# Two MLPs behind an attention: the last product in seven products too, and a weight matrix turned by VectorE

## The chip, the cores and the metric

One core of one Trainium2 chip. The metric is the time of one execution in device microseconds (us), as the median of several runs. A profile is one execution, recorded instruction by instruction; its span runs from the first to the last instruction. The engines have short names in it: PE is TensorE, DVE is VectorE, ACT is ScalarE, POOL is GpSimd, SP is SyncE, which issues nearly all DMAs.

## What is computed

```python
def reference(q, k, v, w_in, w_out, w1, w2, w3, w_out2):
    x = windowed_attention(q, k, v)         # 4 x 8 heads x 576 x 64 -> 2304 tokens x 512
    h = x @ w_in                            # 512 -> 2048
    x = np.maximum(0.01 * h, h) @ w_out     # 2048 -> 512
    a = x @ w1                              # 512 -> 1024
    b = x @ w2
    h = a * b @ w3                          # 1024 -> 1024
    return h @ w_out2                       # 1024 -> 512
```

The inputs q, k and v come in single precision, the weights in double. A product in single precision is made of three matmuls, of high and low parts: with a = a_hi + a_lo, the terms are lo x hi, hi x lo and hi x hi (`mm3`, line 124, matmuls on lines 126 to 128). The high part is a rounding copy and the low part a subtraction, the two steps of `split_steps` (line 115).

## The kernel before

The program goes through stages, each with TensorE work in it. Attention and first MLP share the time up to about 350 us, the first MLP running on to about 550 us. Beside the first MLP's last parts lie two more stages.

**The fold of w3** (about 346 to 432 us). Since (a*b) w3 w_out2 = (a*b)(w3 w_out2), the kernel computes wp = w3 w_out2 once, 1024x512. w3 comes in 16 blocks of 128x512 double-precision words. `conv3` turns each into single precision (POOL, ScalarE and VectorE, tile `wf` with its second half-word in `rf`), and `keep_w3` (line 654) turns it by four TensorE transposes of 128x128 into a PSUM bank (`ps_w3T`, line 661). It is then split into high and low (`w3T`), VectorE making the low part. `split_wo2` (line 640) splits the rows of w_out2 (`wo`), `fold_steps` (line 674) multiplies into four banks `ps_wp`, `store_steps` (line 683) copies these out and stores them in DRAM. The order of all this is written by hand: each letter of the string `START` (line 928) is one step of one stage, emitted on whatever engines it uses, and the string `LOADS` orders SP's loads. The engines run their own queues in that order and meet at semaphores.

**The weight sums** (to about 550 us), `weight_sums`, make for the gates the sums of blocks of w1 and w2 that a 2x2 product in seven products wants, and store them in DRAM (`ws_dram`). `split_wp` (line 777, letters `,` and `;`) splits wp here, 8 times.

**The second MLP** (551.8 us to the end, loop at line 1086) is what the change is about. It runs three passes; a pass has 768 tokens, two chunks of 384. A pass has eight gates. `Gate` (line 784) computes for 128 of the 1024 features both a and b, for both chunks: a 2x2 block product of weights and tokens in seven products rather than eight, numbered 1, 5, 2, 6, 7, 3, 4 in their order. Each has six matmuls 128x384. They read `ys`, seven tiles of token sums and parts for this pass (`sum_y_steps`, line 754; `ysum` a sum, then a split of 128x768), and `ws`, the weight sums. Intermediate sums stay in the banks a, b, c, e; ScalarE copies between them, VectorE does the additions and the product a*b, ScalarE and POOL split the result (`keep`, line 800) into `p`, the stationary operand of the final product. The next gates' first products are emitted between the last products of the gate before.

`final_part` (line 840) is the final product: for each of the 18 token tiles of 128 tokens 8 x 3 matmuls 128x512 (`ps_y`) of p with wp, a copy by ScalarE (line 852) and one DMA of 128 rows of 2 KB (line 854); the last tile goes in two halves of 256 columns. At the end of a pass the sums `ys` of the next pass are emitted two by two between those token tiles.

Of the kernel before, what the change touches and what calls it, by code (L numbers as in the profile page):

```python
# [28 lines left out]
def tile_window_attention_two_mlps(  # L29
# [14 lines left out]
    nc = tc.nc  # L44
# [100 lines left out]

    def shift(w):
        nc.vector.tensor_scalar(w, w, 3, None, op0=ALU.logical_shift_left)
        yield

    def to_float32(raw, w, r, e_t, shifted=False):  # L150
# [4 lines left out]
        yield  # L155
        halves = r.bitcast(I16).rearrange("p (n two) -> p n two", two=2)
# [35 lines left out]
    class Convert:  # L192
# [3 lines left out]
        def __init__(self, jobs, raw_tile, w_tile, r_tile, pats):  # L196
            self.jobs, self.raw_tile, self.w_tile, self.r_tile = jobs, raw_tile, w_tile, r_tile
            self.raws, self.fetched, self.made, self.done, self.pats = {}, 0, 0, None, pats
            self.ws = {}
# [21 lines left out]

        def block(self):
            i = self.made
            self.made = i + 1
            w, r = self.w_tile(i), self.r_tile(i)
            self.ws[i] = w
            e = [engine_of[x] for x in self.pats[i % len(self.pats)]]
            yield from to_float32(self.raws.pop(i), w, r, e[0], shifted=True)
# [362 lines left out]
    def evacuate_steps(c, f, f0, f1):  # L591
        n = CH[c][1]
        x2 = x2_parts(c)
        if f == f1 - 1:
            for i in range(2):
# [11 lines left out]
                else:  # L607
                    for j in range(2):
                        if c == NCH - 1:
                            if j == 0:  # L610
                                st6 = fin.tile([P, 2, MT], F32, tag="p", name=f"st{c}_{i}", bufs=2 * NI)
# [15 lines left out]
    def load_w3(raw, src, i):  # L627

        r0, c0 = i // (NI // NG) * NG * P, i % (NI // NG) * 2 * P
        nc.sync.dma_start(  # L630
            raw.rearrange("p (c f) -> p c f", c=NG),
            src[r0 : r0 + NG * P, c0 : c0 + 2 * P].rearrange("(c p) f -> p c f", p=P),
        )
# [20 lines left out]
    def keep_w3(i):  # L654


        def finish(w, e_hi, e_lo):
            ps = bank(f"ps_w3T{i}")
            for j in range(2):
                for c in range(NG):  # L660
                    nc.tensor.transpose(
                        ps[:, (j * NG + c) * P : (j * NG + c + 1) * P],
                        w[:, (c * 2 + j) * P : (c * 2 + j + 1) * P], ident,
                    )
# [3 lines left out]
            yield from split_steps(  # L668
                t[:, 0], t[:, 1], ps.rearrange("p (j r) -> p j r", j=2), e_hi, e_lo
            )  # L670
# [12 lines left out]
    def store_steps(g):  # L683
        for x in range(NG):
            st = st_t[:, x * 2 * HS[0] :][:, :DM]
            copy_on(nc.scalar if x % 2 else nc.vector)(st, wp_ps[g][x])
# [5 lines left out]
    yf, ys, pr = {}, {}, {}  # L692
# [61 lines left out]
    def sum_y_steps(p, k):  # L754
        b11, b21, b12, b22 = (yf[2 * p + c][:, 2 * a : 2 * a + 2] for c in range(2) for a in range(2))
        s = {0: b11, 2: b21, 4: b22}.get(k)
        if s is None:
            if k == 1:
                ysum[0] = pre.tile([P, 2, MT], F32, tag="ysum", name=f"ysum{p}", bufs=1)
            if k == 5:  # L760
                ysum[1] = fin.tile([P, 2, MT], F32, tag="ysum", name=f"ysum{p}_5", bufs=1)
            s = ysum[k == 5]
# [5 lines left out]
        yield from split_steps(t[:, 0], t[:, 1], s, nc.scalar, nc.vector)  # L768
# [4 lines left out]
    def load_wp(ib):  # L773
        wp[ib] = wo_slot(f"wps{ib}")
        nc.sync.dma_start(wp[ib][:, 1].bitcast(F32), wp_dram[ib * P : (ib + 1) * P, :])

    def split_wp(ib):
        t = wp[ib]
        yield from split_steps(t[:, 0], t[:, 1], t[:, 1].bitcast(F32), nc.scalar, nc.vector)

    def one(tag, name):
        return banks.tile([P, 512], F32, tag=tag, name=name, bufs=2)

    class Gate:
# [3 lines left out]
        def __init__(self, p, i):  # L788
            self.p, self.i = p, i

        def product(self, k, ps, seeded=False):
            x, j, of = PRODUCT[k]
            w = ws[self.p, self.i, x][:, j]
# [3 lines left out]
        def temp(self, name):  # L797
            return fin.tile([P, MT], F32, tag=name, name=f"{name}{self.p}_{self.i}", bufs=2)

        def keep(self, c, g):  # L800
            t = fin.tile([P, 2, MT], F32R, tag="p", name=f"p{2 * self.p + c}_{self.i}", bufs=2 * NI)
            split(t[:, 0], t[:, 1], g, nc.scalar, nc.gpsimd)
            pr[2 * self.p + c, self.i] = t

        def first(self):
            name = f"{self.p}_{self.i}"
            self.a = one("a", f"ps_a{name}")[:, :MT]
            self.product(1, self.a)
            self.b = one("b", f"ps_b{name}")[:, :MT]
            nc.scalar.copy(self.b, self.a)  # L810

        def second(self):
            self.e = one("e", f"ps_e{self.p}_{self.i}")[:, :MT]
# [7 lines left out]
            self.c = one("c", f"ps_c{self.p}_{self.i}")[:, :MT]  # L821
            nc.scalar.copy(self.c, self.b)

        def third(self):
# [9 lines left out]
            self.product(4, self.b, seeded=True)  # L834
            tt(self.c11, self.c11, self.b, op=ALU.mult)
            self.keep(0, self.c11)

    ps_y = {}

    def final_part(c, tb, i0, i1, cols=None):  # L840
        x, n = cols or (0, DM)
        if i0 == 0:
            ps_y[c, tb, x] = one("a", f"ps_y{c}_{tb}_{x}")[:, :n]
        ps = ps_y[c, tb, x]
        for i in range(i0, i1):
            mm3(
# [310 lines left out]
```

## Time and profile before

| | us |
|---|---|
| median of 3 runs (lowest, highest) | 830.77 (830.13, 831.62) |
| the profiled execution | 830.42 |
| its span | 828.6 |
| TensorE busy | 816.0 (98%) |
| VectorE busy | 426.8 (52%) |
| ScalarE busy | 413.2 (50%) |
| POOL busy | 206.4 (25%) |
| share of TensorE in the chain of work that ended last | 93% |

Busy time of TensorE counts matmuls that overlap in the array; what a matmul costs the queue is the distance between two starts. The views by window show the stages, the timeline the starts, and the groups by line and shape the durations on the other engines.

### The profile page before, as it was taken

What the parts mean: (1) busy time and instruction counts of PE and PEld (TensorE: products, weight loads), DVE (VectorE), ACT (ScalarE), POOL (GpSimd) and SP (SyncE); (2) the same over time, 40 slices, a digit from 0 to 9 for tenths busy, and PEclk for the clock granted to TensorE, in tenths of its full rate; (3) what the DMA queues carried; (4) which work ended last, traced back from release to release, by engine and by line L of the source; (5) the groups of instructions that cost most, each with busy time, mean ns of one, the idle gap of its engine ahead of it and who ended that gap; (6) DMA issues with size and microseconds to landing.
All of it is one profiled execution on the core that took longest, in us unless ns stands there. A gap on an engine that the chain in (4) does not pass through costs nothing.

```text
span 828.6 us, 15344 instructions
## 1 busy us (share of the span) xinstructions
PE 816.0 (98%) x5816; PEld 776.9 (94%) x5816; DVE 426.8 (52%) x852; ACT 413.2 (50%) x929; POOL 206.4 (25%) x236
## 2 busy tenths in 40 slices
PE   7999999999999999999999999999999999999998
PEld 6799899999999999989989999999998999899987
DVE  4999997553645364564653768752324233233310
ACT  3899882452134343565654778654423443334411
POOL 4514521333433143422212200002210121002210
PEclk9999999999999999999999999999999999999999
DMA  6995837346444441465746889749731885158001
GB/s 141 274 321 185 264 102 200 99 141 185 109 137 100 100 107 30 156 215 178 228 141 222 271 286 346 246 150 325 255 97 51 326 293 181 44 202 253 22 26 51
DMA packets 104569, 146.37 MB, mean 177 GB/s; under 512 B 44720, under 2 KB 70064, under 8 KB 104496
## 3 DMA queue, kind: packets, MB, share of 16 engines
q1 hardware_dynamic: 104496, 145.39, 55.9%
q8 instruction: 46, 0.75, 0.4%
q14 instruction: 27, 0.22, 0.1%
HBM read 115.87 MB, written 29.49 MB: 175 GB/s over the span
## 4 chain that ended last, share of the span: by engine, by line
PE 93%; SPq 2%; DVE 2%; ACT 1%; issue 1%; DMA 1%; POOL 0%; DVEq 0%; ACTq 0%; POOLq 0%
PE ps_h L126 8%; PE ps_x L126 8%; PE ps_x L127 8%; PE ps_x L128 8%; PE ps_h L128 8%; PE ps_h L127 8%; PE ps_y L128 4%; PE ps_y L127 4%; PE ps_y L126 4%; PE ps_b L128 3%; PE ps_b L126 3%; PE ps_b L127 3%; PE ps_s L402 2%; PE ps_o L488 2%; PE ps_a L126 2%; PE ps_a L128 2%
## 5 line engine op out<-in xcount | busy, mean ns | idle before, releaser
L126 PE MATMUL ps_h<-x,win 128*128 128x384 f32 (+2 forms) x448 | 143.1, 319 | 1.0 <-ACT g L539 1.0
L128 PE MATMUL ps_h<-x,win 128*128 128x384 f32 (+2 forms) x448 | 140.0, 313 | 0.0
L127 PE MATMUL ps_h<-x,win 128*128 128x384 f32 (+2 forms) x448 | 140.0, 312 | 0.0
L126 PE MATMUL ps_x<-gs,wout 128*128 128x384 f32 (+2 forms) x356 | 114.7, 322 | 0.0
L128 PE MATMUL ps_x<-gs,wout 128*128 128x384 f32 (+2 forms) x356 | 112.4, 316 | 0.0
L127 PE MATMUL ps_x<-gs,wout 128*128 128x384 f32 (+2 forms) x356 | 112.4, 316 | 0.0
L118 POOL TENSOR_TENSOR gs<-g,gs 128x384 fp32r<-128x384 f32 (+2 forms) x69 | 65.3, 947 | 147.7 <-DVE gs L116 141.9
L539 ACT ACTIVATE g<-ps_h 128x384 f32<-128x384 f32 (+2 forms) x112 | 49.3, 440 | 104.4 <-PE ps_h L128 67.7
L118 POOL TENSOR_TENSOR p<-u,p 128x384 fp32r<-128x384 f32 x24 | 24.4, 1015 | 270.6 <-ACT p L116 238.8
L126 PEld LDWEIGHTS ps_h<-x,win 128*128 128x128 f32 x448 | 84.6, 189 | 3.3 <-ACT g L539 1.5
L127 PEld LDWEIGHTS ps_h<-x,win 128*128 128x128 f32 x448 | 84.6, 189 | 0.3
L128 PEld LDWEIGHTS ps_h<-x,win 128*128 128x128 f32 x448 | 84.5, 189 | 0.0
L829 DVE TENSOR_TENSOR u<-u,ps_e 128x384 f32<-128x384 f32 x24 | 13.3, 554 | 136.3 <-ACT u L828 136.3
L126 PEld LDWEIGHTS ps_x<-gs,wout 128*128 128x128 f32 x356 | 67.1, 189 | 1.0
L127 PEld LDWEIGHTS ps_x<-gs,wout 128*128 128x128 f32 x356 | 67.2, 189 | 0.2
L128 PEld LDWEIGHTS ps_x<-gs,wout 128*128 128x128 f32 x356 | 67.1, 189 | 0.0
L128 PE MATMUL ps_y<-wps,p 128*128 128x512 f32 (+1 forms) x152 | 57.5, 379 | 0.0
L127 PE MATMUL ps_y<-wps,p 128*128 128x512 f32 (+1 forms) x152 | 57.5, 379 | 0.0
L126 PE MATMUL ps_y<-wps,p 128*128 128x512 f32 (+1 forms) x152 | 57.4, 378 | 0.0
L116 DVE CAST gs<-g 128x384 fp32r<-128x384 f32 (+2 forms) x70 | 24.7, 352 | 62.5 <-PE ps_x L128 52.5
L128 PE MATMUL ps_b<-ys,ws 128*128 128x384 f32 x144 | 48.1, 334 | 0.0
L126 PE MATMUL ps_b<-ys,ws 128*128 128x384 f32 x144 | 48.1, 334 | 0.0
(157 smaller groups left out, 1902.8 us busy)
## 6 DMA issues: line engine op xcount, KB each, us to landing
ws<-ws_dram SPq DMA_DIRECT2D x63, 512.0 KB
raw<-in_moe_w_out_dram SPq DMA_DIRECT2D x24, 512.0 KB
ws_dram<-ws SPq DMA_DIRECT2D x24, 512.0 KB
raw<-in_moe_w_in_dram SPq DMA_DIRECT2D x16, 512.0 KB
rawf<-in_moe_w_dram SPq DMA_DIRECT2D x16, 512.0 KB
wo2f<-wo_dram SPq DMA_DIRECT2D x32, 256.0 KB
rawl<-in_moe_w_dram SPq DMA_DIRECT2D x16, 512.0 KB
q<-in_q_dram SPq DMA_DIRECT2D x48, 140.0 KB
```

The source lines that it names most:

```text
L116: copy_on(e_hi)(hi, src)
L118: e_lo.tensor_tensor(lo, src, hi.bitcast(F32), op=ALU.subtract)
L126: nc.tensor.matmul(ps, a[1], b[0], start=first, stop=False, skip_group_check=seeded)
L127: nc.tensor.matmul(ps, a[0], b[1], start=False, stop=False, skip_group_check=seeded)
L128: nc.tensor.matmul(ps, a[0], b[0], start=False, stop=last, skip_group_check=seeded)
L402: nc.tensor.matmul(ps[j * QB : (j + 1) * QB, i - bl.start], qt[d, i * QB : (i + 1) * QB], kt[d, first_key(i, plain) : first_key(i, plain) ...
L488: nc.tensor.matmul(ps[j * D : (j + 1) * D, i * QB : (i + 1) * QB], vt[i][:, h + j, :], t[:, i, j * QB : (j + 1) * QB], start=True, stop=True,)
L539: nc.scalar.activation(g, ps, AF.Prelu, alpha=SLOPE)
L829: tt(u3, u3, self.e, op=PLUS)
```

## The change

**The final product in seven products.** Each pass is cut into two halves of four gates, and each half's final product is made for two column halves d, as a 2x2 block product (class `Final`): the blocks are the feature halves of a pair of gates (even and odd) by the two chunks on the one side, blocks of wp on the other. Its result stands transposed, output features on partitions and 384 tokens along the row. So the gates keep no longer a*b of two chunks but seven sums of pairs of gates (`Gate.keep` with keys 1 to 7; the differences by VectorE, the low parts of 1, 5, 7, 4, 3 by POOL, of 6 and 2 by VectorE). The first half's results are kept in `yacc` (four tiles) and added in the second half, four additions a half by POOL, the others by VectorE. The output tile is turned back by VectorE's 32x32 transpose and written in pieces of 256 bytes, 384 pieces to a DMA, four DMAs to a tile.

**The parts of wp** for it (`fold_sums`) are sums and splits of four blocks of 256 rows and lie in the first half of the first pass; `split_wp` is gone. Lists `urgent` and `spare` (`behind`, `need`) hold the steps that stand beside the products, one list item being begun behind each product.

**The gates** change a little: bank c is b + m5 by VectorE rather than a copy by ScalarE, u is b + m5 by VectorE. The weights for later gates come in a ring of 16 slots of 256 KB, 16 products ahead.

**w3** is loaded in bands of 32 rows and turned by VectorE's transpose, 16 instructions of 128x512, into `rf`; w_out2 is stored from bands that suit it, and the copies in `store_steps` are cut in two with the columns reordered. `START` and `LOADS` are changed in some letters.

The core of the diff:

```diff
+        for b in range(P // E):
+            nc.sync.dma_start(
+                raw[b * E : (b + 1) * E].rearrange("x (r f) -> x r f", f=2 * E),
+                rows(
+                    src, r0 * F2 + c0 + b * 2 * E,
+                    [[F2, E], [E * F2, NG * P // E], [1, 2 * E]],
+                ),
+            )
...
         def finish(w, e_hi, e_lo):
-            ps = bank(f"ps_w3T{i}")
-            for j in range(2):
-                for c in range(NG):
-                    nc.tensor.transpose(
-                        ps[:, (j * NG + c) * P : (j * NG + c + 1) * P],
-                        w[:, (c * 2 + j) * P : (c * 2 + j + 1) * P], ident,
-                    )
+            turned = conv3.rs[i].bitcast(F32).rearrange("p (j r x) -> p r j x", j=2, x=E)
+            nc.vector.transpose(turned, w.rearrange("p (r j y) -> p r j y", j=2, y=E))
             yield
...
     def sum_y_steps(p, k):
...
+        e_lo = nc.gpsimd if p and k in LO_ON_POOL else nc.vector
...
-        yield from split_steps(t[:, 0], t[:, 1], s, nc.scalar, nc.vector)
+        yield from split_steps(t[:, 0], t[:, 1], s, nc.scalar, e_lo)
+
+    LO_ON_POOL = (0, 2, 4, 5)
...
         def third(self):
             tt = nc.vector.tensor_tensor
             self.product(7, self.b, seeded=True)
             u3 = self.temp("u3")
-            nc.scalar.copy(u3, self.b)
-            tt(u3, u3, self.e, op=PLUS)
+            tt(u3, self.b, self.m5, op=PLUS)
+            behind()
             self.product(3, self.c, seeded=True)
-            tt(self.m5, self.m5, self.c, op=PLUS)
-            tt(u3, u3, self.m5, op=ALU.mult)
-            self.keep(1, u3)
+            behind()
+            tt(u3, u3, self.c, op=ALU.mult)
+            odd = self.i % 2
+            if odd:
+
+                t1, u3e = raw["t1"], raw["u3"]
+                self.keep(6, t1, nc.vector, (t1, u3, t1))
             self.product(4, self.b, seeded=True)
+            behind()
             tt(self.c11, self.c11, self.b, op=ALU.mult)
-            self.keep(0, self.c11)
...
+            if odd:
+                self.keep(2, self.c11, nc.vector)
+                self.keep(7, u3e, nc.gpsimd, (u3e, u3, u3e))
+                self.keep(4, t1, nc.gpsimd, (t1, self.c11, t1))
+                self.keep(3, u3, nc.gpsimd)
+            else:
+                raw["u3"] = u3
+                raw["t1"] = t1 = self.temp("t1", 1)
+                self.keep(1, self.c11, nc.gpsimd)
+                self.keep(5, t1, nc.gpsimd, (t1, u3, self.c11))
...
+        def out(self, src, m, c):
...
+            t = out_t[m, c]
+            nc.vector.transpose(t[:, :, d], src.rearrange("p (t x) -> p t x", x=E))
+            for a in range(P // E) if d == 1 else ():
...
+                queue = nc.scalar if last and (m, c) == (1, 0) and a % 2 else nc.sync
+                queue.dma_start(to, t[a * E : (a + 1) * E].rearrange("y t d x -> y t (d x)"))
...
+        def p5(self):
+            self.e = one("e", f"ps_e{self.name}")[:, :MT]
+            self.product(5, self.e)
+            behind()
+            self.m5 = fin.tile([P, MT], F32, tag="m5", name=f"m5{self.name}", bufs=2)
+            nc.scalar.copy(self.m5, self.e)
+            if self.h == 1:
+                for m in range(2):
+                    nc.gpsimd.tensor_tensor(self.acc(m, 1), self.acc(m, 1), self.m5, op=PLUS)
...
+                y[0].p5()
+                y[1].p1()
+                y[1].p5()
+                for f in ("p6", "p2", "p7"):
+                    for d in range(2):
+                        getattr(y[d], f)()
```

How it stands in the queues, at three places. **VectorE in the fold**, around the seventh and eighth of the rows of w_out2; `wf` and `rf` are the two halves of a block of w3, `wo` the low parts of w_out2, `w3T` those of the turned block, `gs` belongs to the first MLP. First after:

```order
L676 STREAM_TRANSPOSE rf_4854<-wf_4836 128x8x2x32
L118 TENSOR_TENSOR wo_7_7_4926<-wo2f_4874,wo_7_7_4926 128x512
L118 TENSOR_TENSOR wo_8_0_4930<-wo2f_4898,wo_8_0_4930 128x512
L154 TENSOR_SCALAR wf_4932<-wf_4932 128x512
L118 TENSOR_TENSOR w3T_4939<-rf_4854,w3T_4939 128x512
L171 ISA wf_4932<-wf_4932,rf_4946 128x1024
```

A transpose per block stands ahead of the splits, and the split of w3T reads `rf` in SBUF. Before, the same split reads TensorE's bank, here for the first block:

```order
L163 ISA wf_4654<-wf_4654,rf_4655 128x1024
L116 CAST gs<-g 128x384
L118 TENSOR_TENSOR w3T_4733<-ps_w3T_4712,w3T_4733 128x512
L147 TENSOR_SCALAR wf_4730<-wf_4730 128x512
L163 ISA wf_4730<-wf_4730,rf_4731 128x1024
```

Nothing else of VectorE's queue is taken away there.

**VectorE and POOL at the end of a pass** (`ys` and `ysum` for the next pass, `p` the gates' kept parts, `ps_ay`, `ps_cy` the final product's banks, `u_7`, `c_7` the last gate's terms). VectorE before:

```order
L835 TENSOR_TENSOR c_7_7276<-c_7_7276,ps_b_7_7221 128x384
L118 TENSOR_TENSOR ys_0_7380<-yf_6931,ys_0_7380 128x768
L764 TENSOR_TENSOR ysum_7383<-yf_6933,yf_6931 128x768
L118 TENSOR_TENSOR ys_1_7385<-ysum_7383,ys_1_7385 128x768
L118 TENSOR_TENSOR ys_2_7416<-yf_6931,ys_2_7416 128x768
```

The ys come behind the last gate. After, VectorE has them between the gate's own terms:

```order
L931 TENSOR_TENSOR u_7_7507<-ps_b_7_7425,m_7_7465 128x384
L779 TENSOR_TENSOR ysum_7511<-yf_6963,yf_6961 128x768
L935 TENSOR_TENSOR u_7_7507<-u_7_7507,ps_c_7_7487 128x384
L118 TENSOR_TENSOR ys_1_7521<-ysum_7511,ys_1_7521 128x768
L893 TENSOR_TENSOR t_6_7454<-u_7_7507,t_6_7454 128x384
L943 TENSOR_TENSOR c_7_7476<-c_7_7476,ps_b_7_7425 128x384
L118 TENSOR_TENSOR p_3_6_7544<-t_6_7454,p_3_6_7544 128x384
L118 TENSOR_TENSOR p_3_2_7546<-c_7_7476,p_3_2_7546 128x384
L893 TENSOR_TENSOR u_6_7434<-u_7_7507,u_6_7434 128x384
L1072 TENSOR_TENSOR ps_ay_1_1_7552<-ps_ay_1_1_7552,yacc_6910 128x384
```

and POOL, which had only the two splits of the last gate there, has:

```order
L118 TENSOR_TENSOR ys_0_7509<-yf_6961,ys_0_7509 128x768
L118 TENSOR_TENSOR ys_2_7532<-yf_6961,ys_2_7532 128x768
L1082 TENSOR_TENSOR yacc_6911<-yacc_6911,m5y_1_0_7548 128x384
L1082 TENSOR_TENSOR yacc_7091<-yacc_7091,m5y_1_0_7548 128x384
L1082 TENSOR_TENSOR yacc_6911<-yacc_6911,m5y_1_1_7575 128x384
L1082 TENSOR_TENSOR yacc_7091<-yacc_7091,m5y_1_1_7575 128x384
L118 TENSOR_TENSOR p_3_7_7572<-u_6_7434,p_3_7_7572 128x384
L118 TENSOR_TENSOR p_3_4_7586<-t_6_7454,p_3_4_7586 128x384
L118 TENSOR_TENSOR p_3_3_7588<-u_7_7507,p_3_3_7588 128x384
```

**SP at the end of the program.** Before, one DMA a token tile:

```order
L854 DMA out_dram<-o_0_0_8955 128x512
L854 DMA out_dram<-o_1_0_8983 128x512
L854 DMA out_dram<-o_2_0_9011 128x256
L854 DMA out_dram<-o_2_256_9039 128x256
L1152 UNCONDITIONAL_BRANCH
```

After, four a tile of 128 features by 384 tokens by two column halves:

```order
L1062 DMA out_dram<-ot_0_0_9345 32x12x64 x4
L1062 DMA out_dram<-ot_1_1_9380 32x12x64 x4
L1062 DMA out_dram<-ot_0_1_9382 32x12x64 x4
L1062 DMA out_dram<-ot_1_0_9395 32x12x64 x2
L1469 UNCONDITIONAL_BRANCH
```

The other two of the last tile stand on ScalarE's queue.

## Rows read from the trace of the kernel before

**Rows 1.** The page: busy us, share of the span, instructions.

```profile
PE 816.0 (98%) x5816; PEld 776.9 (94%) x5816; DVE 426.8 (52%) x852; ACT 413.2 (50%) x929; POOL 206.4 (25%) x236
```

**Rows 2.** Windows: length, busy us by engine, clock, DMA share, GB/s.

```profile
346.50:432.40 85.90, 85.90 (x463) 77.89 (x462) 51.48 (x86) 50.13 (x87) 21.26 (x24) 1.00 0.64 196
551.80:825.40 273.60, 273.59 (x1464) 257.27 (x1464) 71.77 (x120) 101.27 (x201) 47.64 (x48) 1.00 0.48 165
```

**Rows 3.** Timeline of TensorE in a gate: start, duration, line, tiles.

```profile
557.13 0.33 PE L126 MATMUL ps_b<-ys,ws 128*128 128x384 f32 x1
...
558.00 0.33 PE L128 MATMUL ps_b<-ys,ws 128*128 128x384 f32 x1
```

**Rows 4.** Timeline of TensorE in the final product.

```profile
815.65 0.39 PE L127 MATMUL ps_y<-wps,p 128*128 128x512 f32 x1
...
816.56 0.39 PE L128 MATMUL ps_y<-wps,p 128*128 128x512 f32 x1
```

**Rows 5.** Chain of work in the fold: start, us, what.

```profile
348.80 0.44 PE ps_w3T L661 x4
```

**Rows 6.** Timeline at the start of the second MLP, TensorE and ScalarE.

```profile
551.81 0.44 PE L126 MATMUL ps_a<-ys,ws 128*128 128x384 f32 x1 [1.45 <-ACT st L617]
553.23 0.46 ACT L810 COPY ps_b<-ps_a 128x384 f32<-128x384 f32 x1 [0.24 <-PE ps_a L128]
```

**Rows 7.** Groups of VectorE by shape in the second MLP: count | busy us, mean ns.

```profile
L829 DVE TENSOR_TENSOR u<-u,ps_e 128x384 f32<-128x384 f32 x24 | 13.3, 554 | 136.3 <-ACT u L828 136.3
L118 DVE TENSOR_TENSOR ys<-ysum,ys 128x768 fp32r<-128x768 f32 x9 | 8.6, 958 | 8.1 <-ACT ys L116 8.1
```

**Rows 8.** Groups of ScalarE by shape in the second MLP.

```profile
L116 ACT CAST p<-c 128x384 fp32r<-128x384 f32 x24 | 12.3, 514 | 0.0
L116 ACT CAST ys<-ysum 128x768 fp32r<-128x768 f32 x9 | 7.5, 836 | 11.7 <-DVE ysum L764 11.7
L816 ACT COPY m<-ps_e 128x384 f32<-128x384 f32 x24 | 11.4, 474 | 1.7 <-PE ps_e L128 1.7
```

**Rows 9.** POOL's subtractions on line 118: count, ns min/median/max, forms.

```profile
L118 POOL TENSOR_TENSOR gs<-g,gs x69: 722/889/1437, 122.5 to 477.9; 128x384 fp32r<-128x384 f32 x32, 128x256 fp32r<-128x256 f32 x20, 128x320 fp32r<-128x320 f32 x17
L118 POOL TENSOR_TENSOR p<-u,p x24: 1010/1016/1020, 561.2 to 795.2; 128x384 fp32r<-128x384 f32 x24
```

**Rows 10.** VectorE's transposes on lines 299 and 312, in the same form.

```profile
L299 DVE STREAM_TRANSPOSE qT<-q x6: 1244/1248/1260, 127.4 to 268.9; 128x576 f32<-128x576 f32 x6
L312 DVE STREAM_TRANSPOSE qT<-q x24: 399/419/475, 47.8 to 305.3; 128x160 f32<-128x160 f32 x12, 128x128 f32<-128x128 f32 x12
```

**Rows 11.** Timeline of VectorE, three places in the fold.

```profile
354.78 1.05 DVE L118 TENSOR_TENSOR wo<-wo2f,wo 128x512 fp32r<-128x512 f32 x1 [0.68 <-ACT wo L116]
375.00 0.69 DVE L163 CUSTOM_DVE_ANT_0 wf<-wf,rf 128x1024 uint16<-128x1024 uint16 x1
402.55 0.69 DVE L118 TENSOR_TENSOR w3T<-ps_w3T,w3T 128x512 fp32r<-128x512 f32 x1 [0.69 <-ACT w3T L116]
```

**Rows 12.** Timeline of POOL at the same places.

```profile
354.62 0.67 POOL L113 TENSOR_SCALAR wf<-rawf 128x512 f32<-128x512 f32 x1 [1.27 <-PE ps_w3T L661]
375.23 1.33 POOL L118 TENSOR_TENSOR gs<-g,gs 128x384 fp32r<-128x384 f32 x1 [1.48 <-DVE gs L116]
402.59 1.02 POOL L118 TENSOR_TENSOR gs<-g,gs 128x384 fp32r<-128x384 f32 x1
```

**Rows 13.** The end: timeline of TensorE and ScalarE, SP's issues on line 854.

```profile
825.14 0.28 PE L128 MATMUL ps_y<-wps,p 128*128 128x256 f32 x1
825.50 0.37 ACT L852 COPY o<-ps_y 128x256 f32<-128x256 f32 x1 [2.50 <-PE ps_y L128]
L854 SPq DMA_DIRECT2D out_dram<-o x19: 332/333/338, 619.3 to 825.9; - x19
```

**Rows 14.** DMA queue, 12:18 (256-byte reads) and 444:450: packets, MB, share.

```profile
q1 hardware_dynamic: 3433, 0.84, 62.9%
...
q1 hardware_dynamic: 1717, 2.08, 96.2%
```

**Rows 15.** Groups of VectorE by shape in the fold.

```profile
L118 DVE TENSOR_TENSOR wo<-wo2f,wo 128x512 fp32r<-128x512 f32 x27 | 20.3, 757 | 15.3 <-ACT wo L116 15.3
```

More of the change, by code (lines that the diff above doesn't have):

```diff
@@ L781, in one, with advance, behind, need @@
     def one(tag, name):
         return banks.tile([P, 512], F32, tag=tag, name=name, bufs=2)
+    urgent, spare, in_work, done_keys = [], [], [], set()
+    def advance():
+        for x in list(in_work):
+            if next(x[1], x) is x:
+                done_keys.add(x[0])
+                in_work.remove(x)
+    def behind():
+        advance()
+        queue = urgent or spare
+        if queue:
+            in_work.append(queue.pop(0))
+            next(in_work[-1][1])
+    def need(key):
+        while key not in done_keys:
+            if any(k == key for k, _ in in_work):
+                advance()
+                continue
+            queue = urgent if any(k == key for k, _ in urgent) else spare
+            in_work.append(queue.pop(0))
+            next(in_work[-1][1])
@@ new lines, in tile_window_attention_two_mlps, with ask_ring @@
+    for g in gate_order():
+        if g[0] or g[1] >= NI // 2:
+            ring_n[g] = len(ring_n)
+    ring_order = list(ring_n)
+    def ask_ring():
+        while ring_asked[0] < len(ring_order) and ring_asked[0] < ring_free[0]:
+            n = ring_asked[0]
+            p, i, k = ring_order[n]
+            x, j, _ = PRODUCT[k]
+            at = ((8 * x - 4) * P if x else 0) + j * 4 * P
+            dst = ring[n // 2 % RING][:, n % 2].bitcast(F32).rearrange("p b c d -> p (b c d)")
+            nc.sync.dma_start(dst, ws_dram[i][:, at : at + 4 * P])
+            ring_asked[0] = n + 1
@@ L793, in product @@
[L793 removed]
+            need(("ys", self.p, k))
+            w = weights(self.p, self.i, k)
+            of = PRODUCT[k][2]
             for cc in range(2):
                 mm3(ps, parts(w, cc), parts(ys[of], cc), cc == 0 and not seeded, cc == 1, seeded)
[L797 to L803, printed above, removed]
+            n = ring_n.get((self.p, self.i, k))
@@ new lines, in tile_window_attention_two_mlps, with places, wide @@
+    outs = []
+    def places(i):
+        def wide(q, place):
+            for x in ("sa", "sb"):
+                wpc[x, q] = place(f"wp{x}{q}").rearrange("p a b c d -> p a (b c d)")
+        if i == 0:
+            for q in range(2):
+                wide(q, win_tile)
+                fold_work(q, 2)
+                if q == 0:
+                    fold_work(2, 0)
+        elif i == 1:
+            for x in ("sa", "sb"):
+                wpc[x, 2] = wo_slot(f"wp{x}2")
+            rest(2)
+            fold_work(2, 1, 2)
+            fold_work(3, 0)
+            rest(6)
+            wide(3, win_tile)
+            fold_work(3, 1, 2)
+            for c in range(2):
+                t = win_tile(f"yacc{c}").bitcast(F32).rearrange("p a b c d -> p (a b c d)")
+                yacc[0, c] = t[:, : 2 * MT].rearrange("p (d t) -> p d t", d=2)
+        else:
+            for _ in range(RING // 2):
+                ring.append(win_tile(f"ring{len(ring)}"))
+                ring_free[0] += 2
+            ask_ring()
```

361 lines of the change are left out of this document (260 added, 101 removed).

## The prediction, made before the changed kernel ran

> **What bounds the kernel now.** I read the page first: TensorE is busy for 816.0 of 828.6 us [rows 1]. Busy time alone can deceive, so next come the windows by stage: in the fold of w3 (346.5 to 432.4) and in the whole second MLP (551.8 to 825.4) TensorE is busy in every microsecond, at a granted clock of 1.00, while VectorE has 51.5 of 85.9 us and 71.8 of 273.6, and POOL 21.3 and 47.6 [rows 2]. So what ends last in both stages is TensorE's own queue of matmuls, and the length of its work is the length of the stage. The timeline of TensorE gives the price of one matmul as the distance of starts, not as its duration, since they overlap: five distances between 557.13 and 558.00 make 0.174 us for a 128x384 [rows 3], and four between 815.65 and 816.56 make 0.2275 for a 128x512 [rows 4]; over longer stretches I take 0.1733 and 0.227. The question of this change is therefore twofold: how many such distances go, and whether VectorE, ScalarE and POOL can still deliver what the new products read.
>
> All is reckoned against the profiled execution: 830.42 us with a span of 828.6; the median of the three runs is 830.77. What a measurement here can tell from no change is about 0.2%, 1.66 us.
>
> **A. Fewer matmuls in the second MLP.** The gates' 1008 matmuls stay: 1008 x 0.1733 = 174.7 us. Of the window's 273.6 [rows 2] the final product thus takes 98.9 us now. After, it is 3 passes x 2 halves x 2 column halves x 7 products x 6 matmuls = 504 of 128x384, so 87.35 us. A = -11.5. Both figures are at full clock, and the new products read operands of the same shapes as the gates', so I see no reason for a dearer step.
>
> **B. No transposes by TensorE in the fold.** 16 blocks of four transposes go, each block 0.44 us on the chain [rows 5]: B = -7.0.
>
> **C. Start of the second MLP.** TensorE waits 1.45 us at 551.81 for ScalarE to empty a bank [rows 6]. After, the first two banks come from another pool and the first product starts at once, near 550.2; but product 2 adds into a bank that ScalarE copies first, and that copy (at 553.23 now [rows 6]) still stands behind the same casts. The copy becomes late in place of the bank: C = -0.5 (0 to -1.5).
>
> **D. The ends of the first and second pass.** This is the term that decides. There the sums and splits for the next pass (ys) have so far had 27 us of final product in which TensorE wanted nothing new from VectorE. Now the last half's final products stand there, which need new splits of the gates at once, and the order shows POOL with two ys splits, four additions into yacc and three gate splits in one queue. I walk it instruction by instruction, from t = 0, the end of product 6 of the last gate. TensorE then wants a product each 1.04 us (6 x 0.1733): final product 1 of column half 0, the gate's 7, 3 and 4, final 5, 1, 5, and from 7.3 on 6, 6, 2, 2, 7, 7, 3, 4, 3, 4; undisturbed the last ends at 17.7. Durations: VectorE 0.55 for 384 columns and 0.95 for 768 [rows 7]; ScalarE's casts 0.51 and 0.84 [rows 8], its copies about 0.47; POOL 1.0 for 384, and for 768 some 1.87 by the slope between 256 (0.722 at least) and 384 [rows 9]; VectorE's transpose 0.885 by the slope between 0.42 for 128 or 160 columns and 1.248 for 576 [rows 10].
>
> If the two engines ran side by side, this walk ends at 18.8: a stall of 1.1 us. But the trace shows that they exclude each other. VectorE's 128x512 split of wo takes 1.05 us while POOL has an instruction (at 354.78 and 354.62) [rows 11, 12], its like takes 0.69 with a source in PSUM even beside POOL (402.55 and 402.59), and POOL's split takes 1.33 rather than 1.02 when it meets VectorE's two-operand instruction of 375.00. The loser's work ends about 0.87 us after the winner ends (376.56 against 375.69), so it saves some 0.15 by overlap. With that, the walk goes: POOL splits ys0 from 2.46 to 4.33; VectorE's sum for ys1, which stands ahead of the gate's u*c, therefore ends at 5.1 instead of 3.6, u*c at 5.6; ys1's split ends at 7.0, POOL's ys2 at 8.8, and only then VectorE's t6, its cast and its split: 10.4, where product 6 wanted it at 7.8. TensorE stands 2.6 us. The copies of m5 sit behind those casts on ScalarE, so POOL's four additions run from 11.2 to 16.1, each alternating with a VectorE instruction, and the split for product 7 ends at 17.06: another 2.2 us. The split for 3 ends at 20.4 (1.2), and late copies and sums cost 1.5 in all. TensorE's last product ends at 25.2 instead of 17.7: 7.5 us. Whichever engine wins a tie, the walk gives 7.4 to 7.5. There are two such ends; the third pass has no ys behind it, and the same walk without them gives no stall. **D = +15.0**, with ends of 2.2 (side by side) and 19.3 (no overlap at all, 9.6 each); I take the middle one because the rows on 375 show the 0.15.
>
> [...]
>
> **E. The tail.** Now the last matmul starts at 825.14, its copy runs at 825.50 for 0.37, and one 0.33 us issue later the span ends at 828.6, some 3.2 after the last matmul's end [rows 13]. After, VectorE has six transposes from three products before the end, of which the last comes off the engine 1.9 us after it; behind it SP issues four pieces of one tile and two of the next at 0.33 to 0.48 each, done 3.6 after the end, and the landing takes the 2.4 us that it takes now. 5.9 - 3.2: E = +2.8. The output leaves in pieces of 256 bytes, 1536 to a tile. The trace has such pieces only as reads: 62.9% of 16 engines over 6 us for 3433 packets is 17.6 ns each [rows 14], 1.7 us a tile. Were a piece as dear as the 1.2 KB packets of the other row (54 ns), a tile would take 5.2 us and the last three would lie behind each other: E = +14. Range 1 to 14; I take the value for pieces of the same size.
>
> **F. The fold with VectorE turning w3.** 16 transposes of 128x512, 1.13 us each by the slope of [rows 10], add 18.1 us to VectorE's 51.5 [rows 2] in a stage that shrinks to 78.9: 69.6, 88%. The split of w3T, so far with a PSUM source, now has two SBUF operands and joins those that exclude POOL, as the splits of wo do, whose mean is already 0.757 [rows 15]. Most is hidden by the hidden-layer matmuls of the first MLP, but single blocks will be late: F = +1.5 (0 to 8).
>
> **G. The fold's sums in the first pass.** Eight splits leave the stage before; four sets of sums and splits, some 12 us on VectorE and 8 on POOL, now lie in the first half pass of 43.7 us beside 15 and 10 of the gates. By the exclusion the two together come near 40. A gate's u must be ready one product after its bank: here and there it will not. G = +1.5 (0 to 6). In the other halves I cost the same contest at nothing; the four gate products between cover it.
>
> **Sum.** 830.42 - 11.5 - 7.0 - 0.5 + 15.0 + 2.8 + 1.5 + 1.5 = **832.2 us**. What TensorE is spared comes back as waiting at the two pass ends.
>
> **The rivals.**
> *The engines keep pace* (819.5 to 826): D is 2.2 to 8 because fewer instructions meet than the walk has it. For it: the 768-wide POOL durations are worked out and not seen, and one early split moves all later ones. Against it: all three contests above. With D = 2.2 the sum is 819.4.
> *The fold becomes VectorE's* (slower, 838.7): if VectorE stands for 60% of POOL's 21.3 us there, it needs 69.6 + 12.8 = 82.4 of a stage of 78.9, and with some 4.5 of its waits for casts, TensorE's wait is 8 instead of 1.5. It decides once VectorE is busy for over 95% of the stage. Against it: TensorE has other matmuls to put between.
> *The full lock* (slower, 836.5): D = 19.3.
> *Dear output pieces* (slower, 843): E = 14. In the Trainium skill (DMA: Bandwidth & Descriptors, Specifications) transfers below 512 bytes miss the line rate and are read, modified and written; no row here shows a write of that size, and the reads of 256 bytes do not show it.
>
> **How the numbers follow.** Forecast 0.40 (829 to 836 by the bounds of C, F, G and one us in each walk), engines keep pace 0.36, VectorE-bound fold 0.09, full lock 0.08, dear pieces 0.07. Faster by over 0.2% (under 829.1): nearly all of the second case and a fifth of the first, 0.43. Within 0.2%: under half of the first and a little of the second, 0.19. Slower: the rest, 0.38. Cases of both signs hold most of it, so the range goes from 818, just under the second case, to 840, over the fold's; dear pieces and a D below 1 are left out.
>
> **What would show it.** A: the starts in the second MLP keep 0.173, and there are 1512 matmuls. B: no w3T on the chain in the fold, which ends near 425 plus F. D: in the list of TensorE's waits, 14 to 16 us on splits from VectorE and POOL around two pass ends, POOL's 384-wide additions nearer 1.4 than 1.0. If those waits are under 5 us, the exclusion was mis-weighed. E: last matmul to span end about 6 us. Waits for ring loads would make the forecast wrong in another place: 28 loads of 256 KB per 43.7 us are 168 GB/s, and the queue moved 2.08 MB in 6 us, 347 GB/s, at its busiest [rows 14].

## The result, and the profile after

The changed kernel takes 836.61 us (836.45 to 839.71) against 830.70, medians of four runs each: 5.9 us slower. The ratio is 1.0081 with an interval of 1.0068 to 1.0094. The profiled execution is 836.64 us with a span of 834.9, 6.2 us above the one of before. The page after, its first row against [rows 1]:

```profile
PE 805.8 (97%) x5800; PEld 775.8 (93%) x5800; DVE 525.8 (63%) x1012; ACT 419.2 (50%) x952; POOL 263.7 (32%) x276
```

TensorE is busy for 10 us less and the kernel is 6 us longer: the time is now in TensorE's waits. The windows of the same stages, columns as in [rows 2]: the fold, the second MLP from its first matmul to the end of its last, what follows, and one pass end.

```profile
345.30:436.00 90.70, 86.53 (x424) 75.41 (x423) 65.70 (x110) 52.87 (x93) 22.83 (x24) 1.00 0.65 186
548.90:828.00 279.10, 267.39 (x1514) 262.61 (x1512) 164.05 (x269) 110.83 (x231) 103.14 (x88) 1.00 0.52 163
828.00:834.90 6.90, 0.17 (x1) 0.00 (x0) 0.58 (x1) 0.00 (x0) 0.00 (x0) 0.67 0.75 156
629.00:646.00 17.00, 12.41 (x62) 10.61 (x63) 16.89 (x22) 6.79 (x12) 13.76 (x9) 1.00 0.11 24
```

At the pass end VectorE is busy for 16.9 of 17.0 us and POOL for 13.8, while TensorE has 12.4, overlaps counted in. The list of TensorE's waits up to 650 us, through the second MLP's first pass and its end, names who is late (total, times, longest):

```profile
PE ps_by L127 <- POOL p L118: 1.8, 1, 1.8
PE ps_by L126 <- ACT p L116: 1.8, 1, 1.8
PE ps_cy L127 <- POOL p L118: 1.0, 1, 1.0
PE ps_a L126 <- ACT ps_b L909: 1.0, 1, 1.0
PE ps_by L126 <- DVE ps_by L1102: 0.7, 1, 0.7
```

All but the fourth stand at the pass end. To size it I take starts of matmuls, as in [rows 3], and add up what they are apart beyond 0.1733 us: 1.92, 0.42 and 0.18 at product 6, 1.99 at product 7, 1.15 at product 3, 0.82 at product 4, together 6.5 us, and the same at the second end to 0.02 us. The whole second MLP has 17.0 us of such gaps after its first matmul; before, 0.4.

VectorE and POOL at that end, from their timelines:

```profile
622.57 0.56 DVE L931 TENSOR_TENSOR u<-ps_b,m 128x384 f32<-128x384 f32 x1
623.05 2.36 DVE L779 TENSOR_TENSOR ysum<-yf,yf 128x768 f32<-128x768 f32 x1
625.34 0.54 DVE L935 TENSOR_TENSOR u<-u,ps_c 128x384 f32<-128x384 f32 x1
626.32 0.96 DVE L118 TENSOR_TENSOR ys<-ysum,ys 128x768 fp32r<-128x768 f32 x1 [0.44 <-ACT ys L116]
627.20 2.18 DVE L893 TENSOR_TENSOR t<-u,t 128x384 f32<-128x384 f32 x1
...
622.75 1.85 POOL L118 TENSOR_TENSOR ys<-yf,ys 128x768 fp32r<-128x768 f32 x1 [1.34 <-ACT ys L116]
627.09 1.87 POOL L118 TENSOR_TENSOR ys<-yf,ys 128x768 fp32r<-128x768 f32 x1 [2.49 <-ACT ys L116]
630.84 5.26 POOL L1082 TENSOR_TENSOR yacc<-yacc,m5y 128x384 f32<-128x384 f32 x4 [1.89 <-ACT m5y L1079]
```

POOL's ys 0 ends at 624.60, and VectorE's sum, 0.95 us by itself in the kernel before, only at 625.41; the gate's product with bank c waits behind it. The next difference (t, 0.55 by itself) takes 2.18 behind POOL's ys 2. POOL's four additions take 5.26 us in place of 4.

### The profile page after: what moved, and what is told of

Same layout as the page of the kernel before. It is cut to its first block, busy times and chain, and to the rows that moved or that the text cites. A ratio compares the mean times of both kernels' runs of the same rounds, so it can differ in the third digit from the quotient of the medians.

```text
span 834.9 us, 15947 instructions
## 1 busy us (share of the span) xinstructions
PE 805.8 (97%) x5800; PEld 775.8 (93%) x5800; DVE 525.8 (63%) x1012; ACT 419.2 (50%) x952; POOL 263.7 (32%) x276
## 4 chain that ended last, share of the span: by engine, by line
PE 72%; DVE 13%; ACT 6%; DMA 5%; issue 3%; POOL 1%; SPq 0%; DVEq 0%; ACTq 0%; POOLq 0%
PE ps_x L126 7%; PE ps_x L128 6%; PE ps_x L127 6%; PE ps_h L126 6%; PE ps_h L128 6%; PE ps_h L127 6%; PE ps_b L126 3%; PE ps_b L128 3%; PE ps_b L127 3%; PE ps_s L414 3%; DMA wo2f<-wo_dram 3%; PE ps_a L126 2%; PE ps_a L128 2%; PE ps_a L127 2%; PE ps_o L500 2%
## 5 line engine op out<-in xcount | busy, mean ns | idle before, releaser
L118 POOL TENSOR_TENSOR p<-u,p 128x384 fp32r<-128x384 f32 x24 | 26.1, 1088 | 54.9 <-PE ps_b L128 31.8
L450 ACT ACTIVATE s<-s,nmax 128x96 f32<-128x96 f32 x83 | 30.1, 368 | 23.8 <-DVE nmax L434 23.8
L126 PE MATMUL ps_b<-ys,ring 128*128 128x384 f32 x120 | 40.5, 338 | 0.0
L128 PE MATMUL ps_b<-ys,ring 128*128 128x384 f32 x120 | 40.5, 337 | 0.0
L925 DVE TENSOR_TENSOR ps_c<-ps_b,m 128x384 f32<-128x384 f32 x24 | 13.6, 566 | 42.6 <-PE ps_b L128 40.1
L127 PE MATMUL ps_b<-ys,ring 128*128 128x384 f32 x120 | 40.3, 336 | 0.0
L463 POOL TENSOR_TENSOR s<-s,rec 128x480 f32<-128x480 f32 (+1 forms) x32 | 29.9, 934 | 29.7 <-DVE rec L461 26.2
```

The lines of the kernel that those rows point to most:

```text
L118: e_lo.tensor_tensor(lo, src, hi.bitcast(F32), op=ALU.subtract)
L126: nc.tensor.matmul(ps, a[1], b[0], start=first, stop=False, skip_group_check=seeded)
L127: nc.tensor.matmul(ps, a[0], b[1], start=False, stop=False, skip_group_check=seeded)
L128: nc.tensor.matmul(ps, a[0], b[0], start=False, stop=last, skip_group_check=seeded)
L450: nc.scalar.activation(s[:, i], s[:, i], AF.Exp, bias=nmax[:, i : i + 1], accum_out=total[:, i : i + 1])
L463: nc.gpsimd.tensor_tensor(s, s, rec[:, :nb].unsqueeze(2).to_broadcast([P, nb, KB]), op=ALU.mult)
```

## Experiments

**The work of the pass end left out.** Theory: the two stalls are the ys steps in VectorE's and POOL's queues. Rival: the gate's own splits and POOL's additions are late by themselves.

```diff
-                            for k in range(NM):
-                                key = next(q for q in PRODUCT if PRODUCT[q][2] == k)
-                                spare.append((("ys", p + 1, key), sum_y_steps(p + 1, k)))
+                            done_keys.update(("ys", p + 1, key) for key in PRODUCT)
...
-                    if (h, i) == (0, 1) and p + 1 < NPC:
-                        load_y(2 * p + 2)
-                        load_y(2 * p + 3)
```

The loads of the next pass's tokens go with the steps that read them.

> The token sums ys of the second and third pass are left out (all three passes use those of the first, so two thirds of the output are of the wrong tokens); all else as in the changed kernel. If the stalls at the two pass ends come from the ys steps that stand in the queues of VectorE and POOL there and exclude each other, all of them go: two times 6.5 us in the gaps of TensorE, 836.6 - 13 = 823.6, down to 821 if the small gaps around them go too. If the gate's own late splits and the additions on POOL are the cause, the stalls stay for the greater part: 832 or more.

Measured 823.06 us (821.51 to 825.67), 0.9908 of before: the first number. TensorE's gaps in the second MLP are 2.3 us in all, and VectorE has 9.5 us at the pass end. (The windows of 629 to 646 here and below stand at the same time after the span's start; the second MLP begins 0.8 to 2.1 us later in these runs than in the change.)

```profile
629.00:646.00 17.00, 17.00 (x100) 17.00 (x99) 9.54 (x18) 3.66 (x8) 5.84 (x6) 1.00 0.41 96
```

Shown: the ys steps with their loads cost 13.5 us, and with them away the change would be a gain of 7.6.

**The same work, all of it on VectorE.**

```diff
-    LO_ON_POOL = (0, 2, 4, 5)
+    LO_ON_POOL = ()
```

> The low parts of ys 0, 2, 4, 5 of the next pass made by VectorE (0.96 us each) in place of POOL (1.87). Exclusion of the two engines: the walk of the pass end gives 8.2 us in place of 7.5, since the work that VectorE gains is what it waited for before: about the same, 836 to 839. If instead POOL's own length of queue is what is late (no exclusion), three quarters of POOL's early work is gone and the stall at an end falls from 6.5 to under 3: 829 or less.

Measured 833.91 (833.40 to 835.17), 2.7 us less than the change. The gaps of an end are 0.3, 2.4, 1.2 and 0.4: 4.3 us rather than 6.5. Neither number was met: the walk had the wrong sign, the rival too large a gain. VectorE spends 0.96 us on a split that keeps POOL for 1.87, and that can hold VectorE up as long. I put the walk's wrong sign down to the order of VectorE's queue, which I had set by hand for this variant; no run shows that. The walk places waits; it does not rank variants that are 1 us apart.

**The same work, behind the gate's.**

```diff
+                            rest(4)
                             for k in range(NM):
```

> Four empty places are put ahead of the seven ys steps in the list of side work, so that the last gate's splits, its differences and POOL's additions stand ahead of ys on every engine; nothing is added or left out. Theory (what is late is not the amount of work but that ys stands ahead of what TensorE wants first, and that both engines exclude each other): of 6.5 us an end at most 1 to 2 are left, then at the first products of the next pass: 826 to 829. Rival (the two engines together have too much to do in these 18 us, whatever its order): the wait moves to the first gate of the next pass and keeps its size: 835 to 838.

Measured 840.35 (838.39 to 843.20). The gaps in the final products are gone, and one of 6.4 us stands at the next pass's second product. So the wait moves and keeps its size, as the rival has it, but by a queue that I had not thought of: ScalarE's copy into bank b stands behind the casts of ys, which wait for VectorE's sums. ScalarE and TensorE there:

```profile
643.80 0.83 ACT L116 CAST ys<-yf 128x768 fp32r<-128x768 f32 x1 [2.76 <-DVE yf L779]
645.13 0.83 ACT L116 CAST ys<-ysum 128x768 fp32r<-128x768 f32 x1 [0.50 <-DVE ysum L779]
645.87 0.47 ACT L909 COPY ps_b<-ps_a 128x384 f32<-128x384 f32 x1
...
646.39 0.69 PE L126 MATMUL ps_a<-ys,ring 128*128 128x384 f32 x1 [6.23 <-ACT ps_b L909]
```

The time is above the rival's 835 to 838, and 3.7 us above the change. Behind each of the two waits TensorE ran for some microseconds at the lower clock, which cost 1.8 us each (see the last section): 3.6 us, without which the time would be 836.8.

**The same work, spread.** The first sum and ys 0 begin three products earlier; ys 1 to 3 come behind the gate, ys 4 to 6 later still; only ys 0 is left to POOL.

```diff
-    LO_ON_POOL = (0, 2, 4, 5)
+    LO_ON_POOL = (0,)
...
+                        if h == 1 and i + 2 == last and p + 1 < NPC:
+                            spare.append((("ysum", p + 1), first_sum_steps(p + 1)))
+                            spare.append((("ys", p + 1, 1), sum_y_steps(p + 1, 0)))
...
-                            for k in range(NM):
+                            rest(2)
+                            for k in (1, 2, 3, 4, 5, 6):
+                                if k == 4:
+                                    rest(5)
```

> The ys work of a pass end is kept whole but spread: the first sum and ys 0 are begun three products before the last gate's end, ys 1 to 3 behind the gate's splits, ys 4 to 6 so late that the next pass's first copy on ScalarE stands ahead of their casts; the low parts of ys 2, 4, 5 are VectorE's. Theory (the stall is the order on in-order queues that exclude each other; the run with ys moved behind only shifted it to that copy on ScalarE): at most 1.5 us an end are left, so 836.6 - 10 = 826.6, 825 to 829. Rival (there is too much work for both engines around the end, whatever the order): some 5 us an end stay, at another place: 833 to 837.

Measured 829.78 (827.73 to 832.55), 0.9984 of before (0.9971 to 0.9997). An end has gaps of 1.5, 0.4 and 0.8: 2.7 us of 6.5. So a changed order on the in-order queues and less work on POOL, both changed by this run, take away 3.8 us of the stall. Less was gained than expected, since 2.7 and not 1.5 remain at each end.

**Two of POOL's additions to VectorE as well**, on top of the spread run:

```diff
-                    nc.gpsimd.tensor_tensor(self.acc(m, 1), self.acc(m, 1), self.m5, op=PLUS)
+                    e, src = (nc.vector, self.e) if m else (nc.gpsimd, self.m5)
+                    e.tensor_tensor(self.acc(m, 1), self.acc(m, 1), src, op=PLUS)
```

> The run with ys spread, and of POOL's four additions into yacc two made by VectorE straight from the PSUM bank (one SBUF operand, so no exclusion). In the spread run 1.9 us an end remain as waits on POOL's splits of the gate for products 7 and 3, which stand behind the additions, and 0.8 on VectorE at the next pass's first sum. Theory of the queues: POOL's 2 us less take away most of the 1.9, VectorE's 1.1 more adds to the 0.8: 829.8 - 2 = 828, 827 to 829. If VectorE is what is full there, nothing is gained: 829.5 to 831.

Measured 827.37 (826.20 to 829.72), 0.9963 of before (0.9948 to 0.9977): the fastest version here that computes the right output. The windows of the pass end, of the spread run and of this one:

```profile
629.00:646.00 17.00, 15.42 (x87) 14.78 (x87) 16.28 (x24) 6.60 (x12) 8.19 (x7) 1.00 0.27 59
```

```profile
629.00:646.00 17.00, 15.88 (x88) 14.85 (x87) 16.58 (x27) 7.41 (x13) 5.37 (x4) 1.00 0.39 85
```

VectorE is recorded as busy as in the change, 16.6 of 17 us, and TensorE waits 1.5 us an end. That counts time behind POOL, as in the 2.36 us above for a sum of 0.95, so it does not tell a full engine from a blocked one. In a row, the gaps of an end are 6.5 us in the change, 4.3 with POOL's ys splits moved to VectorE and the order kept, 2.7 with ys 0 back on POOL and the order changed, 1.5 with two additions less on POOL. So 3.4 of the 5.0 us came where work left POOL, and 1.6 with the order. The changed order with all of POOL's splits kept was not run, so how much order alone can do stays open.

**The fold: TensorE's transposes put back.** Loads and turning of w3 as before, all else as changed.

```diff
-            nc.vector.transpose(turned, w.rearrange("p (r j y) -> p r j y", j=2, y=E))
...
+                    nc.tensor.transpose(
+                        ps[:, (j * NG + c) * P : (j * NG + c + 1) * P],
+                        w[:, (c * 2 + j) * P : (c * 2 + j + 1) * P], ident,
+                    )
...
```

> w3 loaded and turned as before (four TensorE transposes a block into a PSUM bank, 512 KB loads), the order of the letters and all of the second MLP as in the changed kernel. Theory: TensorE has its 7.0 us of transposes back, and its 6.5 us of gaps in the fold go: 836.6 + 0.5 = 837.1, so 836 to 838. Rival (the gaps in the fold come from the changed order and from the loads in the other stages, not from the turning): the gaps stay and 7.0 are added: 843.5.

Measured 840.18 (839.74 to 840.30), between the two numbers. The fold's gaps fall from 7.3 to 2.5 us, of which 1.6 is one wait; before, with its own letters, they were 0.8. The one wait is of `ps_h`, for the bank that TensorE's transposes fill and VectorE's split reads, a bank that the change does not need; without it 0.9 us are left, as before. So between 4.8 and 6.4 us of the gaps belong to VectorE's turning, and little to the changed order.

**VectorE's turning alone, in the kernel before**, with the loads and the letters of the fold that belong to it.

```diff
-            ps = bank(f"ps_w3T{i}")
...
+            nc.vector.transpose(turned, w.rearrange("p (r j y) -> p r j y", j=2, y=E))
```

> The kernel before with only w3 turned by VectorE (loads in bands and the fold's part of the letters as in the changed kernel, second MLP as before). From the traces: TensorE loses 7.0 us of transposes and gets 6.5 us of gaps, so 830.7 - 0.5 = 830.2, down to 829.4 by the earlier start of the second MLP. From the run with TensorE's transposes put back into the changed kernel, which was 3.5 us longer: 827.2.

Measured 829.92 (829.25 to 830.77), 0.9986 of before (0.9976 to 0.9995), with 7.5 us of gaps in the fold. The first number is right: 7.0 us of matmuls are traded for 6.7 of waits.

**What makes the fold's gaps.** Three edits of the change and one of before:

```diff
-            turned = conv3.rs[i].bitcast(F32).rearrange("p (j r x) -> p r j x", j=2, x=E)
+            ps = bank(f"ps_w3T{i}")
+            turned = ps.rearrange("p (j r x) -> p r j x", j=2, x=E)
...
```

> VectorE's transpose of w3 writes into a PSUM bank in place of the tile rf, and the split reads it there, as with TensorE before; nothing else. That takes away two waits of the fold: the next block's second words no longer wait for the split that reads rf, and the split no longer has two SBUF operands. If these make the fold's 7.3 us of gaps, they fall to the 2.5 of the run with TensorE's transposes: 836.6 - 4.8 = 831.8, 831 to 833. If the gaps come from the transpose's place in VectorE's in-order queue behind splits of wo that wait for their casts, they stay: 835.5 to 837.

Measured 836.87 (834.71 to 838.56), gaps 7.8 us: the second number. But the gaps are not all the same ones:

```profile
PE ps_wp L126 <- DVE w3T L118: 2.5, 3, 1.7
PE ps_h L126 <- DVE w3T L118: 2.2, 1, 2.2
```

In the change all the larger gaps stand ahead of `ps_wp`. Here 2.6 us stand ahead of `ps_h`, which waits for the bank that the turned block now takes, and the others come to 5.2. The change's own fold has 6.6 to 8.4 us of gaps in the six traces that contain it. So the tile rf held longer and the split's second SBUF operand are not most of it; as a part of it the run does not rule them out.

```diff
-    FOLD_CONV = ("GAD",)
+    FOLD_CONV = ("AAD",)
```

> The scaling of w3's high words (16 instructions of 128x512) by ScalarE in place of POOL; all else as in the changed kernel. If the exclusion of VectorE and POOL is what makes the splits in the fold late (their means are 0.75 to 0.76 rather than 0.69), the gaps shrink by 1 to 2 us: 834.5 to 835.5. If it is the chain from cast to split through ScalarE and VectorE, ScalarE's 10 us more in the same stage lengthen it: 837 or more.

Measured 844.16 (842.00 to 845.65), 7.6 us longer than the change: POOL out of VectorE's way helps nothing, and ScalarE's load in the same chain costs. The gaps are 12.7 us; 1.6 of them are the clock, granted at 0.57 from 353 to 357 us behind the longest wait. TensorE's waits for w3T in the fold there (total, times, longest):

```profile
PE ps_wp L126 <- DVE w3T L118: 5.1, 6, 2.6
```

The third, on top of the spread run, moves each transpose ahead of the splits of wo in VectorE's queue, by moving the letter 4 in `START` behind the letter 3:

```diff
-            ...Jc2l2L3LH3Hgc4gJl0561d2Wc3LlWpr4pLH05r61L2d45gW0L36W...
+            ...Jc2l2L3LH34HgcgJl0561d2Wc344LlWprpLH05r61L2d5gW0L36W...
```

> The run with ys spread over the pass end, and in the fold each transpose of w3 moved ahead in VectorE's queue, directly behind the last joining of words (letter 4 behind letter 3), in front of splits of wo that wait for ScalarE's casts. If the transposes' place in the in-order queue makes the fold's gaps (some 7 to 8 us in every kernel with VectorE's transposes), they halve: 829.8 - 4 = 826. If the length of the chain cast, split, matmul is what counts, with the casts at their old places on ScalarE, the time stays within 1 us of 829.8.

Measured 829.08 (827.69 to 830.75), 0.7 less than the spread run and within its scatter, gaps 7.6 against 8.4: the place of the transpose alone is not it. The last takes the loads by themselves, in the kernel before:

```diff
-        nc.sync.dma_start(
-            raw.rearrange("p (c f) -> p c f", c=NG),
-            src[r0 : r0 + NG * P, c0 : c0 + 2 * P].rearrange("(c p) f -> p c f", p=P),
-        )
+        for b in range(P // E):
+            nc.sync.dma_start(
...
```

> The kernel before, with the loads alone changed: w3 in bands of 32 rows, four DMAs a block in pieces of 512 bytes, and w_out2 from the bands that belong to it; TensorE turns w3 as before (so the rows and columns of w3 come out permuted and the output is not the reference's). If the fold's gaps in the kernels with VectorE's transposes come from the loads (more packets, and the loads of wo's rows late behind them on SP), they appear here too: 830.7 + 3 to 6. If they come from VectorE's extra instruction in the chain of a block, nothing changes: 830.2 to 831.2.

Measured 831.28 (830.31 to 832.41), 1.0008 of before (0.9999 to 1.0018), gaps 0.8 as before: the loads by themselves are not it.

What is left is the chain itself. At the longest gap of the change, timelines of VectorE, ScalarE and TensorE:

```profile
411.92 0.69 DVE L118 TENSOR_TENSOR wo<-wo2f,wo 128x512 fp32r<-128x512 f32 x1 [1.19 <-ACT wo L116]
412.53 0.70 DVE L676 STREAM_TRANSPOSE rf<-wf 128x512 f32<-128x512 f32 x1
413.16 0.65 DVE L118 TENSOR_TENSOR wo<-wo2f,wo 128x512 fp32r<-128x512 f32 x1
413.92 0.94 DVE L118 TENSOR_TENSOR w3T<-rf,w3T 128x512 fp32r<-128x512 f32 x1
...
411.27 0.62 ACT L116 CAST wo<-wo2f 128x512 fp32r<-128x512 f32 x1 [1.40 <-DMA wo2f<-wo_dram]
412.17 0.62 ACT L116 CAST wo<-wo2f 128x512 fp32r<-128x512 f32 x1 [0.28 <-DMA wo2f<-wo_dram]
413.27 0.62 ACT L116 CAST w3T<-rf 128x512 fp32r<-128x512 f32 x1 [0.48 <-DVE rf L676]
...
414.91 0.50 PE L126 MATMUL ps_wp<-wo,w3T 128*128 128x512 f32 x1 [1.34 <-DVE w3T L118]
```

A wo cast waits for its load, VectorE's split of it waits for the cast, the transpose stands behind that split, the cast of w3T behind the transpose, its split behind that and behind another split of wo: each engine waits for the other with a queue behind it. VectorE is busy for 65.7 of 90.7 us. That the length of this chain is the cause fits these runs; it is argued from them and not shown, and which link would have to go was not found.

One link stands out that none of these runs takes away. In the chain of work from 345 to 440 us the loads of rows of w_out2 (`wo2f`, two buffers) have the largest share after; before, TensorE's matmuls have nearly all of it:

```profile
by line: PE ps_wp L128 15.6%; PE ps_wp L127 15.5%; PE ps_wp L126 15.4%; PE ps_h L128 8.9%; PE ps_h L126 8.7%; PE ps_h L127 8.6%; PE ps_w3T L661 7.4%; PE ps_x L126 6.8%; PE ps_x L128 6.6%; PE ps_x L127 6.6%
by line: DMA wo2f<-wo_dram 22.4%; DVE wo L118 12.9%; issue 10.5%; ACT wo L116 7.1%; DVE w3T L118 6.1%; DVE rf L676 5.4%; ACT rf L167 4.6%; ACT rf L165 4.0%; DMA x_dram<-st 3.5%; ACT w3T L116 2.6%; PE ps_x L126 2.2%; DVE st L699 2.2%; PE ps_
```

ScalarE's casts wait 6.5 us for these loads after and 1.5 before. In the run with the loads alone they wait 7.6 us and TensorE loses nothing, so a late row reached TensorE only together with VectorE's transposes. A third buffer for the rows was not tried.

## Why the prediction was right or wrong

The forecast was 832.2 in a range of 818 to 840; measured 836.6, on the slower side, which had 0.38 where faster had 0.43, and just outside the 829 to 836 of the forecast's own case. By its steps:

- **A, right.** From 548.9 to 828.0 are 279.1 us; less 17.0 of gaps, 262.1, and 1512 x 0.1733 is 262.0.
- **B, right:** no transposes of TensorE, 7.0 us of its work gone; what it was worth is F's matter.
- **C, right:** the gap at the start is 1.13 us in place of 1.61.
- **D, right in mechanism, a little large.** 6.5 us an end against 7.5. The walk had 2.6 at product 6, 2.2 at 7, 1.2 at 3 and 1.5 for the rest; measured 2.5, 2.0, 1.15 and 0.8. Two durations in it were estimates: POOL's 768-wide split (1.87 by the slope, 1.85 and 1.87 measured) and VectorE's transpose of 384 columns (0.885 by the slope, 0.55). POOL's additions take 1.3 us each, and the third pass's end has no gap over 0.12, both as put. The 0.15 of overlap held: the sum ends 0.81 us after POOL and takes 0.95 alone. The Trainium skill (SBUF — State Buffer, Who interferes with whom) says that a VectorE instruction with two SBUF inputs contends with a POOL instruction that reads SBUF; the trace agrees, with 2.36 us for that sum of 0.95. That the time is the one of the rival with the full lock is chance; D was 13.0, not 19.3.
- **E, a little small:** the last matmul ends at 828.17 and the span at 834.9, 6.7 us against 3.2, so +3.5 in place of +2.8. SP's issues take 0.485 us at the median, the top of the 0.33 to 0.48 that was put; the last starts at 831.7 and ends some 0.4 later than put, and the landing takes some 0.3 more. A write of 256 bytes costs about what the reads of [rows 14] cost: in the last 6.9 us 4388 of them take 75% of 16 engines, 18.9 ns each, against 17.6. By the byte that is 1.7 times the 54 ns for 1.2 KB, but by the piece no extra price shows, and the rival with dear pieces falls.

```profile
827.83 0.34 PE L128 MATMUL ps_by<-p,wpb 128*128 128x384 f32 x1
L1062 SPq DMA_DIRECT2D out_dram<-ot x46: 315/485/738, 640.1 to 831.7; - x46
...
q1 hardware_dynamic: 3588, 0.88, 61.8%
q10 hardware_dynamic: 800, 0.20, 13.2%
```

- **F, the step that failed.** +1.5 was put; the fold's gaps are 7.3 us against 0.8 before, +6.5. It was sized by VectorE's busy share and by the hope of other matmuls between. Neither sets it: the transposes take even less than put (0.70 rather than 1.13), VectorE's share is 72%, and still single blocks came late, several times over; with the turning alone in the kernel before, 7.0 us of matmuls went and 6.7 of waits came. What was missing is the wait of each block for a chain over DMA, ScalarE and VectorE; that its length is the cause is argued above. The rival with a VectorE-bound fold had the size, 8, and the wrong condition, a share over 95%. The group after, against [rows 15]:

```profile
L118 DVE TENSOR_TENSOR wo<-wo2f,wo 128x512 fp32r<-128x512 f32 x29 | 21.6, 752 | 9.4 <-ACT wo L116 9.2
L118 DVE TENSOR_TENSOR w3T<-rf,w3T 128x512 fp32r<-128x512 f32 x16 | 12.0, 748 | 3.3 <-ACT w3T L116 3.0
L676 DVE STREAM_TRANSPOSE rf<-wf 128x512 f32<-128x512 f32 x16 | 11.2, 702 | 0.0
```

- **G, wrong in the good sense:** after C's gap none over 0.12 us in the first pass before its end.
- **Left out:** 2.9 us of gaps under 0.12 each in the second MLP, 0.4 before. With the ys steps left out 1.2 of them remain; why is open.

With the measured terms -11.5 - 7.0 - 0.5 + 13.0 + 2.5 + 3.5 + 6.5 = +6.5, where the profiled executions differ by 6.2. The total came as near as 4.4 us in part by luck: F, the small gaps and E were put 8.2 us too low together, D and G 3.5 too high.

## What to carry to other kernels

Where TensorE's work is cut in a kernel that it bounds, list for each new product what it reads and who stands ahead of that on VectorE, ScalarE and POOL; a walk instruction by instruction with durations from the trace placed each wait here within 0.7 us. A step that comes off a bound engine and becomes one more hop between in-order queues need not be paid in busy time: here VectorE had 72% and the turning was paid for in waits, so follow the chain of a block, its loads included, and not the share. When two engines exclude each other, moving work to the one that looks idle can cost both: here taking splits off POOL for a VectorE that was recorded as full won 2.2 of 6.5 us an end, and a changed order on top of it 1.6 more.

## What the runs showed that was not expected

After a long wait the granted clock of TensorE can fall to 1.2 GHz for some microseconds. In the run with ys behind the gate, around the 6.4 us wait:

```profile
640.00:646.30 6.30, 0.16 (x1) 0.00 (x0) 5.97 (x7) 3.03 (x6) 3.43 (x2) 0.77 0.00 0
646.30:650.30 4.00, 3.90 (x12) 3.91 (x13) 2.24 (x3) 0.93 (x3) 0.47 (x1) 0.51 0.81 176
650.30:654.00 3.70, 3.70 (x23) 3.70 (x23) 1.45 (x3) 0.46 (x1) 0.00 (x0) 1.00 0.96 248
```

The share of 0.51 is the lower of two levels, 1.2 of 2.4 GHz. Twelve matmuls have starts 0.32 us apart instead of 0.173, so the wait costs 1.8 us more than its length. It does not come each time: a wait of 2.8 us in the fold of the spread run had no such tail, one of 2.1 in that of the version with the additions moved had; the waits at the pass ends had none in the profile of the change. VectorE's 32x32 transposes are cheaper by the element in blocks of this form than in [rows 10]: 0.70 us for 128x512 and 0.55 for 128x384, where the others take 1.25 for 128x576.
